# A second fold of the sequence axis in a Fourier mixing, weight loads issued by SyncE, and a new written-out order for the first part

## The chip, the cores and the metric

One Trainium2 chip; the kernel runs on one of its cores. A core has TensorE (PE, the matrix unit), VectorE (DVE), ScalarE (ACT), GpSimd (POOL) and SyncE (SP, which only issues transfers here). The metric is the device time of one execution in microseconds, lower is better; a profiled execution gives a trace beside it.

## What is computed

Two blocks in a row, all in float32. The first is an attention without a softmax over positions (8 batches, 8 heads, 576 positions, head size 64, 128 random features); its output is read as x with 8 batches of 576 rows of 512 columns. The second mixes x by a two-dimensional Fourier transform, of which the real part is kept, and ends in a two-layer perceptron.

```python
def phi(x):
    h = einsum('bhsd,md->bhsm', x, omega) - sum(x * x, -1) / 2
    return exp(h - max(h, -1)) / sqrt(m)
num = phi(q_s) @ (phi(k_s).T @ v);  x = num / (phi(q_s) @ sum(phi(k_s)) + 1e-06)
u = x + real(fft(fft(x, axis=1), axis=2))
un = (u - mean(u)) / sqrt(var(u) + 1e-06)
out = u + maximum(un @ w_ch1, 0) @ w_ch2
```

## The kernel before

The program has two parts. The **first part** does attention, mixing, the narrowing of the two weight matrices (they arrive as float64 and are rebuilt as float32) and the perceptron for the first 512 rows (four "plain" tiles of 128 rows); it also prepares sums of the weights. The **second part** does the perceptron for the other 4096 rows in eight blocks of 512 by a Strassen-like scheme with seven products for eight (L1130 for the first layer, L1309 for the second).

*Attention* runs over 32 pairs of heads (from L512). For each pair q and k are loaded by SP (L347, L350) into two buffers, v into three (L355). PE transposes them (L470) and multiplies them by omega in four 64x64 quarters of its array (L544). DVE takes the maxima (L488), ACT the exponentials e (L505). PE forms the products of the k features with v in quarters (L578), transposes the q features (L470), whose copies qeT ACT takes out of PSUM (L477), and multiplies them by the result in two column halves (L621, L629). DVE adds epsilon, takes the reciprocal and divides (L638, L639, L641) into the tile x of the batch: five slots of 128 partitions, each for two of the nine residues of the position modulo 9, with residue 0 in slot 4 on both partition halves. Three such streams of pairs run interleaved.

*Mixing* of a batch (from L653) starts when its four pairs are in x. The real part of the transform is a cosine product minus a sine product, so rows t and 576 - t are first added for the cosines and subtracted for the sines (L668), then columns in two steps (L670, L674, L687, L694). That leaves three chunks of rows, `fold`. On PE each of four sets (cosine and sine, even and odd columns) contracts the three chunks with a table of 320 frequencies (L712: 12 products of 128x320 a batch); ACT copies each set out of its one PSUM bank (L722). For three groups of rows follow the products over the columns (L739) and the middle column (L744); ACT and DVE take the differences and sums out (L760, L765, L768), and DVE adds one mirror half to x, POOL the other (L776, L777). The results go to a DRAM tensor `us` per batch (L785), the mirrored ones to `uh` (L782), from where one transfer per batch copies them in reverse order into `us` (L803).

```python
for c in range(NC3):
    nc.tensor.matmul(
        yp[:, 0:NK], lhsT=fold[:, c, n, :], rhs=tab[:, c, :],
        start=(c == 0), stop=(c == NC3 - 1),
    )
```

*Weights*: 32 pieces of 512 KB are issued from POOL's queue (L434) into four slabs. For each piece ACT or POOL scales the high words (L409, L407), DVE takes sign and mantissa apart in four instructions (L411, L413, L416, L418), POOL adds the low part (L420).

*Plain tiles*: rows of `us` are read back by SP, normalised on DVE, POOL and ACT (L853 to L867, transposes on PE in L863), multiplied by the first weights (L924), rectified by ACT or DVE (L908, L910), multiplied by the second (L947), and added to u (L960). In the rows' order in `us` the nine residues follow one another, and each 128-row tile is written out by two transfers.

**What sets the order.** Every step is listed as a `Step`: the engine or engines that may do it, a cost, what it waits for, and the buffers and PSUM banks it takes and gives back. `Listing.run` (L159, with `start`, L132) keeps a list of the next step of every stream. For the first part the string `PICKS` says with one character per step which stream is next; where a step names several engines, the one that ends first by the listed costs takes it. For the second part, which has no such string, the step with the earliest start by the listed costs is taken. Each engine then runs its instructions strictly in that order, and SP issues its transfers in that order, waiting where a buffer isn't free.

Of the kernel before, what the change touches and what calls it, by code (L numbers as in the profile page):

```python
# [3 lines left out]

# [9 lines left out]
AF = mybir.ActivationFunctionType  # L14
ALU = mybir.AluOpType
# [12 lines left out]
SLOTS = {1: (0, 0), 2: (1, 0), 3: (0, 1), 4: (1, 1), 8: (0, 2), 7: (1, 2), 6: (0, 3), 5: (1, 3)}  # L28
SLOTS[0] = (0, 4)
# [8 lines left out]
RATE = 190.0  # L38
HOP = 0.15

TURN = 0.1
WIDTH = {"bank": 1, "duo": 2}
FMAX = float(np.finfo(np.float32).max)
# [5 lines left out]
    "00e2ede0ebed3dedebfcdcddfeede3fdfhbi8cdefdebfdgafaggec9hddk0kiij2jejgj7lfffffhcdfffdfcggjehegfi7gjbl"  # L49
    "hbhkjgkkdihfhi7hci7bfiadgkhhjce9didbhhb7gggbfihbbf97acbhbeghefaie8bc7chhhcgfc7cedddh9dd1ccdfif8eggih"  # L50
    "f6g8ejihichdihidfkhfhgjckgigh6eihggiddebd6dcg9eei7cfhei6ddfgihhj78gmkmiidaggjfigdmlg6khhjcj6agghifgg"
    "kh6afejekjkjfigji6j8hjjjiilcj9iegcigdhllkmldjmkkf9j80lca5m7bdai6gfikjaljkika6lhjggic9feikeejhgjij5d7"
    "ldjeafedkdeikjje5g5ielfafej6egkicg8dffgikghjijiee7eeifaaeefhefehdeh7iffd6hb7eeidiedhggiijbkj35fjkjhk"
    "kfgfhkk3h795g4e4i6khchlijigkjji4hlfjfd8lfhlg4mi64bfgjjedjgibk6ijj5cgcijhicgi6lii9fi9lf6ggdijf6bgd8fe"
    "icddchifajihj9fgihgjgi6jbhi6degcbg48ffgfh6ii5kjigihf7jgf9ejggafji7gf7egdfh6ficd6dbhfeeh5addfh5be5bff"
    "c48gai8hg9ageefcj5j7gh6haeeghhjikiehi5mg6lghhl5jjhagd5nglkmlccnjldj9llj45lkjjaemh6gbmlf8f7hgekef6hke"
    "87cldljj8bkhihbhhdc6ffgadkdf7ad5kdbgjhhig6lgcel5mdjedilaidedejihgjegi5ggjhcf5dgc5c775kccdh489j8ddgff"
    "h8cbdgiejkkechjhkkki5gj7kgjjjjfjjjh4i7dhhjjfi4k4h4kjchehg6ihk975g5bfejcehg3dgmggiej6m55bf9igig5h66gg"
    "jjjfiieifh8ege5kdihdlhiheief9k5fimhmcio8hgk7fge5jhgdeifagbgbjeeekhgclgigh7ge8fgefddfaci4icdffhgfid8f"
    "gjffhgihd6gc6cjeelgf3af8hbiccgchgfebg5c9d6ehdfcfeeagghffbhc6f9egchggh6aeehfeekjccbdfafdf50h0gcgabgea"  # L60
    "7fcdcfabg6be8bd4c9dcdcdbcebe6bcgb6cefbacadfeaca7dcdcdchdf9abca66f8dcbd8b98c8aa9c8dd2eabcc87a7b758697"
    "a27277ba9688848aa89a99992b98aa9a287a888729d8a993ba8ac9788aede65bdaacb69ba8ba659b54387a986aaa9baccade"
    "ad9b7bfcecffffde79fe9e6h9bgc3gc3be1eac26e7ebeddbdfeefegd6cdfed2ddf3dadeb3e3cc9dc6c5dbbdcab7b3c72b79b"
    "acbb8abbb679a6a9bb9ab49c7b38a93caa998888888888899888686981458778888888888888841933648786583b59691776"
    "a7c67267761bb4bcb6cc9a679a8aaba3f94df49cbaa675793a9aa88778388a88a93995aa39b94a4954585536126424112222"
    "3333533555523346545266421330442216087635433437704543770334535754155544556455155414437756241426224444"
    "1112032232202111100"
# [39 lines left out]
class Listing:  # L107
# [4 lines left out]
    def __init__(self, buffers):  # L112
        self.free = dict.fromkeys((PE, ACT, DVE, POOL, SP, NONE, PORT), 0.0)
        self.buffers = {name: [0.0] * n for name, n in buffers.items()}
        self.made = {}
        self.moved = 0.0
        self.mode = "whole"
        self.banks = [0.0] * 8
        self.got = None
# [12 lines left out]
    def start(self, step, ready, before):  # L132

        queued = before in step.engines and len(step.engines) == 1
        t = ready[0] if queued else ready[1]
# [15 lines left out]

        def begin(e):
            return max(t, self.free[e] if e != NONE else 0.0, self.free[PORT] if step.on_port(e) else 0.0)

        eng = min(step.engines, key=lambda e: begin(e) + step.engines[e])
        t = begin(eng)
        return t + (TURN if eng == PE and step.mode != self.mode else 0.0), eng

    def run(self, streams, picks=None):  # L159
        todo = []  # L160
        picks = iter(picks or ())

# [14 lines left out]
        while todo:  # L177
            pick = next(picks, None)
            best = None
            for item in todo if pick is None else [todo[int(pick, 36)]]:  # L180
                got = self.start(*item[2:])
                if got is None:
                    continue
                key = got[0] + item[2].bias, item[0]
                if best is None or key < best[0]:
                    best = key, got, item
# [11 lines left out]
            done = end + step.late + (HOP if eng != NONE else 0.0)  # L198
            if step.kb:
                self.moved = max(self.moved, end) + step.kb / RATE  # L200
                done = max(done, self.moved + 1.6)
            for name in step.take:
                if name in WIDTH:
                    n = WIDTH[name]
                    i = self.banks_at(n, begin)[0]
                    self.banks[i : i + n] = [math.inf] * n
                    self.got = Banks(tuple(range(i, i + n)))
                else:
                    self.buffers[name].remove(min(self.buffers[name]))
# [13 lines left out]
def _tables(S, DM):  # L223
# [3 lines left out]
    g, p = np.divmod(np.arange(128), 64)  # L227
    t = np.stack([9 * p + 2 * c + g + 1 for c in range(NL)] + [9 * p], axis=1)
    k = np.concatenate([t[:, c] for c in range(NL)] + [t[:64, NL]])
    w = np.ones(t.shape)  # L230
    w[64:, NL] = 0.0
    turn = (t[:, :, None] * k) % S
    ang = 2.0 * np.pi * turn / S
    cs = np.cos(ang) * w[:, :, None]
    sn = np.where(turn * 2 % S == 0, 0.0, np.sin(ang)) * w[:, :, None]
# [18 lines left out]
def kernel(  # L254
# [19 lines left out]
    NK = NL * 128 + 64  # L274
    KD = DM // 2 + 1
# [48 lines left out]
        bmp=2, slab=4, u=2, unT=1, ht=NFC, ur=1, **{f"vd{i}": 1 for i in range(NV)},  # L324
# [39 lines left out]
    om = att.tile([128, 2, D], F32, name="om", tag="om", bufs=1)  # L364
    for i in range(2):
        nc.sync.dma_start(om[:, i, :], omega[:, :])
# [30 lines left out]
    def narrow(i, dst, raw):  # L397
# [6 lines left out]
        step = Step({ACT: 0.72, POOL: 1.4}, after=(("raw", i),), port=True, bias=1.11)  # L404
# [3 lines left out]
        else:  # L408
            nc.scalar.activation(out=dst, in_=hif, func=AF.Copy, scale=2.0**-112)  # L409
        yield Step(DVE, 0.43, port=True, bias=0.19)  # L410
        nc.vector.tensor_scalar(hi, hi, 0x80000000, None, op0=ALU.bitwise_and)  # L411
        yield Step(DVE, 1.15, port=True, bias=0.36)
        nc.vector.scalar_tensor_tensor(  # L413
            bits, bits, 3, hi, op0=ALU.logical_shift_left, op1=ALU.bitwise_or
        )
        nc.vector.tensor_scalar(hi, bits, 0xFF800000, None, op0=ALU.bitwise_and)  # L416
        yield Step(DVE, 0.7, port=True, bias=-0.99)
        nc.vector.scalar_tensor_tensor(lof, lo, 2.0**-52, hif, op0=ALU.mult, op1=ALU.mult)  # L418
        yield Step(POOL, 1.3, makes=("w", i), give=("slab",), port=True, bias=1.25)
        nc.gpsimd.tensor_tensor(out=dst, in0=dst, in1=lof, op=ALU.add)  # L420

    def weights():
# [4 lines left out]
        for i, (dst, src) in enumerate(parts):  # L427
            if src.dtype == F32:
                yield Step(POOL, 0.6, 4.5, makes=("w", i), kb=256)
                nc.gpsimd.dma_start(dst, src)  # L430
            else:
                yield Step(POOL, 0.6, 5.6, take=("slab",), makes=("raw", i), kb=512)
                raw = slabs.tile([128, CV, 2], U32, name="raw", tag="slab")
                nc.gpsimd.dma_start(raw[:].rearrange("p n two -> p (n two)"), src.bitcast(U32))  # L434
# [6 lines left out]
    us = [dram.tile([S, DM], F32, name=f"us{b}") for b in range(B)]  # L441
    uh = [dram.tile([NL * P, DM], F32, name=f"uh{b}") for b in range(B)]

    def first():

        yield Step(NONE, 3.0)
        yield Step(PE, 0.4, take=("bank",))
        b, omps = got()
        nc.tensor.transpose(omps[:, 0:128], om[:].rearrange("m i d -> m (i d)"), ident[:])
        yield Step(DVE, 0.3, makes="om2", give=(b,))  # L450
        nc.vector.tensor_scalar(om2[:], omps[:, 0:128], SCALE, None, op0=ALU.mult)

    def transposed(src, name, groups, after, makes, give, back=None):
# [3 lines left out]
        for j0, j1 in groups:  # L457
# [3 lines left out]
                0.11 * m,  # L461
# [9 lines left out]
            yield Fork(evicted(dst, b, j0, j1, makes, (j0, j1) == back))  # L471
        return dst

    def evicted(dst, b, j0, j1, makes, back):
        yield Step(ACT, 0.15 + 0.115 * (j1 - j0), 0.1, makes=makes + (j0,), give=(b,), bias=0.08)
        ps = psum_of(b)[:, 0 : 128 * (j1 - j0)].rearrange("q (c p) -> q c p", p=128)
        nc.scalar.activation(  # L477
            out=dst[:, j0:j1, :], in_=ps[:, :, ::-1] if back else ps, func=AF.Copy
        )

    def softmax(n, ts, num, b, es):
# [3 lines left out]
        yield Step(DVE, 0.15 + 0.27 * num, bias=-0.56)  # L485
# [10 lines left out]
        for i, one in enumerate(b):  # L496
            if num == 4 or not i:
                yield Step(
                    ACT, 1.18 if num == 4 else 0.65, 0.0, take=(size,),
# [12 lines left out]
    def attn(n):  # L512
# [16 lines left out]
        def pairs_of(js, *ts):  # L529
# [4 lines left out]
                0.235 * len(js),  # L534
# [52 lines left out]
        def keep():  # L587
            step = Step({DVE: 0.3, ACT: 0.35}, take=("kv",), give=(kvb,), makes=("kv", n))
# [10 lines left out]
            lambda r: feature(R + r),  # L599
            "qeT",  # L600
            ((0, 1), (1, 5), (5, R)),
            lambda j0, j1: tuple(("e", n, t) for t in sorted({place(R + j)[0] for j in range(j0, j1)})),
            ("qeT", n),
            lambda j0, j1: {1: ("e1",), 5: (), R: ("e", "e")}[j1],
            (5, R),
        )
        yield Step(
            PE,
            1.23,
# [5 lines left out]
        ndb, ndp = got()  # L615

        for i, order in enumerate(((2, 1, 4, 3, 7, 8, 5, 6), (2, 1, 4, 3, 7, 8, 5, 6))):
            for r in order:
# [828 lines left out]
```

## Time and profile before

Three runs took 1225.72 us in the median (1225.62 to 1227.41); the profiled execution's span is 1222.5 us, its mean granted TensorE clock 0.997.

| engine | busy us | share of the span | instructions |
|---|---|---|---|
| PE | 1188.2 | 97% | 12705 |
| PE weight loads | 1064.3 | 87% | 12705 |
| DVE | 746.0 | 61% | 1522 |
| ACT | 458.2 | 37% | 1432 |
| POOL | 383.5 | 31% | 451 |

Some groups that the change touches, with busy time and mean duration of one record:

| line, engine, what | count | busy us | mean ns |
|---|---|---|---|
| L712 PE products with the cosine and sine tables | 192 | 56.1 | 440 |
| L744 PE middle column | 144 | 15.3 | 236 and 192 |
| L641 DVE division into x | 32 | 26.4 | 825 |
| L505 ACT exponentials | 576 | 158.9 | 396 |
| L477 ACT copies qeT, 512 and 128 columns | 64 and 32 | 36.5 and 9.3 | 612 and 289 |
| L722 ACT copies y | 32 | 14.1 | 442 |
| L420 POOL sum of the weights' two parts | 32 | 43.7 | 1367 |
| L434 POOL issue of the weight loads | 32 | 19.0 | 594 |
| L668 DVE and POOL first fold | 12 and 4 | 15.2 and 9.4 | 1265 and 2348 |

How to read it: a float32 product of PE shows as two records, so L712's 96 products are 192. Records of PE overlap, so that the mean duration is longer than the spacing of two in a row; busy time counts overlap once. The kernel's page also has the chain of work that ended last, followed back from the last instruction: 92% of the span lies on PE there. L1130 and L1309 have 32% and 29% of it, L712 has 4%.

### The profile page before, as it was taken

The numbers are of one execution on the slowest core, as the hardware profiler recorded it, in microseconds if no ns is written. First come the engines' busy times: TensorE is split into PE (matmuls) and PEld (weight loads), VectorE is DVE, ScalarE is ACT, GpSimd is POOL, SyncE is SP. The second block draws the span as 40 slices with busy tenths as digits, with TensorE's granted clock in tenths as the row PEclk, the third lists the DMA queues.
The fourth block names the chain that finished last, engine by engine and source line by source line (L and its number), as shares of the span: only waits on it lengthen the run. The fifth ranks groups of instructions, "written<-read, shape, count | busy, mean of one in ns | idle before, by whom it ended". The sixth has DMA issues, their size and how long they took to land.

```text
span 1222.5 us, 31614 instructions
## 1 busy us (share of the span) xinstructions
PE 1188.2 (97%) x12705; PEld 1064.3 (87%) x12705; DVE 746.0 (61%) x1522; ACT 458.2 (37%) x1432; POOL 383.5 (31%) x451
## 2 busy tenths in 40 slices
PE   6989899999999999999999999999999999999997
PEld 5778878878878777999899899899899899899897
DVE  4889899897674664384384285185276266267255
ACT  6867767666653521222222212222222222222211
POOL 3443443531111013322422422431431521431421
PEclk9999999999999999999999999999999999999999
DMA  9564654736653334195196096186186277267255
GB/s 262 155 205 146 200 177 144 218 91 210 175 194 130 123 114 162 55 304 168 35 304 188 10 309 186 30 284 193 50 258 201 59 248 218 61 212 255 61 175 172
DMA packets 149058, 206.02 MB, mean 169 GB/s; under 512 B 49328, under 2 KB 62896, under 8 KB 148912
## 3 DMA queue, kind: packets, MB, share of 16 engines
q1 hardware_dynamic: 144224, 187.15, 49.8%
q0 software_dynamic: 4608, 16.78, 4.3%
q8 instruction: 101, 1.65, 0.6%
q14 instruction: 45, 0.37, 0.1%
q10 hardware_dynamic: 80, 0.07, 0.0%
HBM read 172.23 MB, written 35.91 MB: 170 GB/s over the span
## 4 chain that ended last, share of the span: by engine, by line
PE 92%; DVE 3%; ACT 3%; DMA 0%; issue 0%; SPq 0%; DVEq 0%; ACTq 0%
PE banks L1130 32%; PE banks L1309 29%; PE banks L924 5%; PE banks L947 5%; PE banks L470 4%; PE banks L544 4%; PE banks L712 4%; PE banks L578 3%; PE banks L621 3%; ACT e L505 2%; PE banks L739 2%; PE banks L863 1%; DVE nmx L488 1%; PE banks L744 1%; ACT kqT L477 1%; PE banks L629 1%
## 5 line engine op out<-in xcount | busy, mean ns | idle before, releaser
L1116 DVE CUSTOM_DVE_ANT_0 hid<-banks,s 128x256 f32<-128x256 f32 x192 | 79.7, 423 | 254.9 <-PE banks L1130 254.9
L1309 PE MATMUL banks<-wl,sums 128*128 128x128 f32 x1792 | 220.3, 275 | 0.0
L1309 PEld LDWEIGHTS banks<-wl,sums 128*128 128x128 f32 x1792 | 210.5, 192 | 1.0
L505 ACT ACTIVATE e<-banks,nmx 128x128 f32<-128x128 f32 x576 | 158.9, 396 | 42.4 <-DVE nmx L488 42.4
L1144 ACT ACTIVATE s<-banks 128x256 f32<-128x256 f32 x192 | 73.6, 383 | 257.6 <-PE banks L1130 257.6
L1130 PE MATMUL banks<-unT,w 128*128 128x256 f32 x704 | 167.3, 379 | 0.0
L1130 PEld LDWEIGHTS banks<-unT,w 128*128 128x128 f32 x704 | 132.7, 190 | 17.9 <-issue 0.5
L1284 ACT ACTIVATE s<-banks 128x128 f32<-128x128 f32 x168 | 46.5, 277 | 236.9 <-PE banks L1309 175.5
L1130 PE MATMUL banks<-tt,w1s 128*128 128x256 f32 x512 | 126.3, 379 | 0.0
L1197 POOL TENSOR_TENSOR hs<-hid 128x256 f32<-128x256 f32 x64 | 46.4, 726 | 200.2 <-DVE hid L1116 173.6
L1130 PEld LDWEIGHTS banks<-tt,w1s 128*128 128x128 f32 x512 | 97.2, 190 | 13.3
L488 DVE TENSOR_REDUCE nmx<-banks 128x8 f32<-128x1024 f32 (+1 forms) x96 | 88.3, 953 | 32.2 <-PE banks L544 27.2
L1309 PE MATMUL banks<-wl,hid 128*128 128x128 f32 x768 | 98.9, 275 | 0.0
L1309 PEld LDWEIGHTS banks<-wl,hid 128*128 128x128 f32 x768 | 94.0, 192 | 1.4 <-DMA wl<-w2l 0.2
L1289 DVE TENSOR_TENSOR part<-banks,s 128x128 f32<-128x128 f32 x168 | 48.7, 290 | 75.3 <-PE banks L1309 74.2
L1197 POOL TENSOR_TENSOR hs<-hid,hs 128x256 f32<-128x256 f32 x64 | 46.4, 725 | 118.7 <-issue 93.3
L544 PE MATMUL banks<-om,kqT 64*64 64x128 f32 x2304 | 76.8, 275 | 4.7 <-ACT kqT L477 2.0
L1130 PE MATMUL banks<-unT,w1s 128*128 128x256 f32 x320 | 80.7, 379 | 0.0
L544 PEld LDWEIGHTS banks<-om,kqT 64*64 64x64 f32 x2304 | 63.8, 134 | 16.1 <-issue 4.2
L857 POOL TENSOR_TENSOR rstd<-rstd,mhalf 128x1 f32<-128x1 f32 x36 | 29.0, 806 | 153.6 <-DVE rstd L855 137.8
L1309 PE MATMUL banks<-wl,hs 128*128 128x128 f32 x576 | 74.9, 275 | 0.4 <-DVE part L1289 0.4
L420 POOL TENSOR_TENSOR w<-w,raw 128x512 f32<-128x512 f32 x32 | 43.7, 1367 | 99.5 <-DVE raw L418 80.5
(115 smaller groups left out, 1998.1 us busy)
## 6 DMA issues: line engine op xcount, KB each, us to landing
wl<-w2l SPq DMA_DIRECT2D x392, 256.0 KB, 3.7
raw<-in_moe_w_ch_dram POOLq DMA_DIRECT2D x32, 512.0 KB, 5.2
kq<-in_k_dram SPq DMA_DIRECT2D x32, 288.0 KB, 3.8
kq<-in_q_dram SPq DMA_DIRECT2D x32, 288.0 KB, 4.5
vd<-in_v_dram SPq DMA_DIRECT2D x32, 288.0 KB, 4.9
out_dram<-ur SPq DMA_DIRECT2D x68, 128.0 KB, 2.4
u<-us SPq DMA_DIRECT2D x32, 256.0 KB, 4.0
ur<-us SPq DMA_DIRECT2D x32, 256.0 KB, 3.1
```

Of the source, the lines that this page charges most:

```text
L470: nc.tensor.transpose(ps[:, (j - j0) * 128 : (j - j0 + 1) * 128], src(j), ident[:])
L488: nc.vector.tensor_reduce(nmx[:, :, 0:num], pps[:, :, 0 : MF * num].rearrange("p b (c m) -> p b c m", m=MF), axis=AX.X, op=ALU.max, negate ...
L505: nc.scalar.activation(out=e[:, c + (i if num == 1 else 0), :], in_=pps[:, i, MF * c : MF * c + MF], func=AF.Exp, bias=nmx[:, i, c : c + 1],)
L544: nc.tensor.matmul(pps[cols, c, MF * m : MF * m + MF], lhsT=kqT[rows, j, cols], rhs=om2[rows, :],)
L712: nc.tensor.matmul(yp[:, 0:NK], lhsT=fold[:, c, n, :], rhs=tab[:, c, :], start=(c == 0), stop=(c == NC3 - 1),)
L924: nc.tensor.matmul(hp[:, 0:TP], lhsT=w1[:, dc, 128 * fc : 128 * fc + 128], rhs=unTs[key][:, dc, :], start=(dc == 0), stop=(dc == NDC - 1),)
L947: nc.tensor.matmul(yp[:, 0:DM], lhsT=hs[fc][:, 128 * i : 128 * i + 128], rhs=w2[:, fc, :], start=(fc == 0), stop=(fc == NFC - 1),)
L1116: nc.vector._custom_dve(TENSOR_ADD_SAT, out=o, in0=ps, in1=sb, s0=FMAX, s1=0.0)
L1130: nc.tensor.matmul(ps[:, 0:HT], lhsT=left(dc), rhs=right(dc), start=start and dc == 0, stop=(dc == D2 - 1), skip_group_check=True,)
L1144: nc.scalar.activation(out=s[:], in_=ps[:, 0:HT], func=AF.Copy)
L1197: nc.gpsimd.tensor_tensor(out=o, in0=l, in1=r, op=op)
L1309: nc.tensor.matmul(ps[:, 0:128], lhsT=left[:, f], rhs=wls[j, i, n][:, f], start=start and f == 0, stop=(f == 3), skip_group_check=True,)
```

## The change

- **Tables and mixing.** After the first fold (t with 576 - t) the two chunks that hold the residues are also added and subtracted (new L740), which pairs t with 288 - t: even frequencies need only the sum, odd ones only the difference. `h` grows by a chunk. The cosine and sine tables get 160 columns for each of sum and difference and 320 for residue 0. Four sets become two groups that take two PSUM banks each; a group has four products of 128x160 and two of 64 rows by 320 columns, one on each half of the array's rows. ACT copies a group out in three pieces. The middle column takes four small products of 64 (or 32) output rows.
- **Attention.** qeT's copies put the positions into the order that the new fold needs; each of the three becomes two ACT instructions with more dimensions. The division may be done by ACT as ten scaled copies.
- **Row order.** `us` is one tensor with the rows in their natural order; results are written there with strides, mirrored ones by eight reversed transfers a batch for one. Tiles of 128 rows are contiguous when they are read and written out.
- **Weights.** The loads move from POOL's queue to SP's; the signs get a tile of their own; the last sum may run on DVE. Omega is loaded from ACT's queue.
- **Order.** A `Clock` holds the constants of the listing, one set for each part; many listed costs of the first part have new values. `PICKS` is new, and a character from the upper range also says that the step goes to the other engine than the one that would end first. First folds, last folds and final sums may each run on DVE or POOL.

```diff
-            for c in range(NC3):
+            plus = slice(0, HK), slice(HK, NK)
+            for m in range(2):
+                for c, cols in ((0, plus[1 - n]), (NL, plus[n])):
+                    nc.tensor.matmul(
+                        yp[:, m, cols],
+                        lhsT=fold[:, c, 2 * n + m, :],
+                        rhs=tab[:, cols],
...
+            for m in range(2):
+                rows = slice(64 * m, 64 * m + 64)
                 nc.tensor.matmul(
-                    yp[:, 0:NK],
-                    lhsT=fold[:, c, n, :],
-                    rhs=tab[:, c, :],
+                    yp[:, m, 0:NK],
+                    lhsT=fold[rows, 1, 2 * n + m, :],
+                    rhs=tab[rows, NK : 2 * NK],
...
+            step = Step({DVE: 0.9, POOL: 1.5}, port=True)
+            yield step
+            eng = nc.gpsimd if step.eng == POOL else nc.vector
+            for dst, o in ((NC3, ALU.add), (1, ALU.subtract)):
+                eng.tensor_tensor(
+                    out=h[:, dst, 0 : 2 * QD + 1],
+                    in0=h[:, 0, 0 : 2 * QD + 1],
+                    in1=h[:, 1, 0 : 2 * QD + 1],
+                    op=o,
+                )
...
-                yield Step(POOL, 0.6, 5.6, take=("slab",), makes=("raw", i), kb=512)
+                yield Step(SP, 0.5, 4.2, take=("slab",), makes=("raw", i), kb=512)
                 raw = slabs.tile([128, CV, 2], U32, name="raw", tag="slab")
-                nc.gpsimd.dma_start(raw[:].rearrange("p n two -> p (n two)"), src.bitcast(U32))
+                nc.sync.dma_start(raw[:].rearrange("p n two -> p (n two)"), src.bitcast(U32))
...
-        nc.sync.dma_start(om[:, i, :], omega[:, :])
+        nc.scalar.dma_start(om2d[:, D * i : D * i + D], omega[:, :])
...
+        step = Step({DVE: 0.74, ACT: 1.2}, give=(ndb,), makes=("x", b, pr), bias=-0.07)
+        yield step
+        if step.eng == ACT:
+            for i in range(2):
+                for c in range(5):
+                    nc.scalar.activation(
+                        out=dst[:, i, c], in_=nd[:, i, c, 0:D], func=AF.Copy, scale=rden[:, i, c : c + 1]
+                    )
+            return
...
-            nc.vector.tensor_scalar(hi, hi, 0x80000000, None, op0=ALU.bitwise_and)
+            nc.vector.tensor_scalar(sign[:], hi, 0x80000000, None, op0=ALU.bitwise_and)
...
-        yield Step(POOL, 1.3, makes=("w", i), give=("slab",), port=True, bias=1.25)
-        nc.gpsimd.tensor_tensor(out=dst, in0=dst, in1=lof, op=ALU.add)
+        step = Step({POOL: 1.25, DVE: 0.61}, makes=("w", i), give=("slab",), port=True, bias=1.25)
+        yield step
+        eng = nc.gpsimd if step.eng == POOL else nc.vector
+        eng.tensor_tensor(out=dst, in0=dst, in1=lof, op=ALU.add)
...
-            for i in range(NC3):
+                g, odd = divmod(i, 2)
+                rows = slice(64 * odd, 64 * odd + 64) if g else slice(0, 128)
+                k1 = HK * odd + k0 + NK * g
                 nc.tensor.matmul(
-                    ab[0:np_, 1, KD : KD + 1],
-                    lhsT=cs[:, i, rows],
-                    rhs=mid_t[:, i, :],
+                    ab[w * odd : w * odd + w, 1, KD : KD + 1],
+                    lhsT=cs[rows, k1 : k1 + w],
+                    rhs=mid_t[rows, 1 if g else NL * (1 - odd), :],
...
+                nc.sync.dma_start(uh[b][:, 2 - slot], u)
...
-            nc.sync.dma_start(
-                us[b][nh : 2 * nh, :].rearrange("t (i d) -> i t d", i=4),
-                uh[b][nh - 1 :: -1, :].rearrange("t (i d) -> i t d", i=4),
-            )
+            for s in range(2):
+                for n, r in enumerate(MIRROR):
+                    back = uh[b][4 * (1 - s) + n].rearrange("e t (i d) -> (e t) i d", i=4)
+                    nc.sync.dma_start(
...
```

## The prediction, written before the changed kernel was run

> **What bounds the kernel now.** I read first the page's busy shares in 40 slices, then the busy time of each engine by stage, then the chain of work and PE's waits. The change touches only what is issued before the first L1130 (464.27 us in the chain), so the stages are cut there. Columns: busy us (instructions) of PE, its weight loads, DVE, ACT, POOL; then clock, DMA share, GB/s.
>
> ```profile
> 0.00:8.00 8.00, 1.69 (x6) 1.05 (x7) 0.29 (x1) 1.88 (x2) 4.23 (x15) 1.00 0.67 211
> 8.00:50.00 42.00, 36.05 (x965) 31.49 (x966) 29.88 (x48) 33.95 (x117) 12.83 (x12) 1.00 0.89 242
> 50.00:100.00 50.00, 44.47 (x957) 38.77 (x956) 44.25 (x87) 37.17 (x118) 22.63 (x21) 0.97 0.60 173
> 100.00:150.00 50.00, 45.48 (x921) 39.40 (x919) 45.42 (x91) 36.33 (x118) 21.06 (x21) 1.00 0.58 171
> 150.00:200.00 50.00, 45.94 (x924) 40.06 (x925) 46.64 (x97) 36.24 (x113) 19.35 (x18) 1.00 0.54 162
> 200.00:464.27 264.27, 263.62 (x3899) 210.18 (x3900) 189.56 (x400) 141.95 (x459) 59.81 (x58) 1.00 0.49 155
> 464.27:1215.00 750.73, 750.35 (x5037) 702.94 (x5037) 389.19 (x800) 170.65 (x507) 243.57 (x309) 1.00 0.54 170
> ```
>
> PE is the bound: it lacks 0.4 us in the last 750 us and 0.65 us from 200 to 464. Only before 200 us does it stand idle, 6.3 us in the first row and 20.1 in the next four; in those four DVE is busy 166.2 of 192 us. The waits of PE name what ends that idle time (total us, times, longest us):
>
> ```profile
> PE banks L470 <- ACT e L505: 6.5, 7, 1.9
> PE banks L449 <- DMA om<-in_omega_dram: 3.5, 1, 3.5
> PE banks L578 <- ACT e L505: 3.2, 4, 1.4
> PE banks L470 <- DMA kq<-in_k_dram: 2.1, 1, 2.1
> ```
>
> ACT's exponentials (L505) wait in turn on DVE's maxima (L488; 42.4 us in the table of waits). So early on a ring PE, DVE, ACT sets the pace; later PE alone. The chain (start, us, what) gives prices for the products of the mixing:
>
> ```profile
> 52.65 3.43 PE banks L712 x12
> ...
> 56.95 3.23 PE banks L712 x12
> ...
> 62.49 0.56 PE banks L744 x6
> ...
> 65.64 0.30 PE banks L744 x6
> ...
> 106.32 1.81 PE banks L712 x6
> ...
> 109.55 1.62 PE banks L712 x6
> ```
>
> One f32 product is two records. Six L712 records last 1.62 us, but 1.81 right after L578's 64x64 products (L544 too, at 206.06): a change of array shape costs 0.19.
>
> **What the Trainium skill says.** "TensorEngine Tiling (Array Packing)", Key Properties: tiles of the array run in parallel, and changing the tiling mode drains TensorE. The trace agrees with both: 32 records of L544 (eight sets of four 64x64 tiles) take 1.03 us, 0.129 a set, where one whole 128-column record (L1309, 16.25/144) takes 0.113; and the 0.19 above. Its Gotcha 1 says that row tiles write different PSUM banks, which the new half-row products do; no product of 64 rows by 128 columns is in this trace. "SBUF — State Buffer", two separate sides: DVE (two SBUF inputs) and GpSimd exclude each other for a whole instruction. The trace agrees: L777 on DVE is 0.42 us in the median, 2.59 at most, beside GpSimd's L776 and L777. So moving work from DVE to GpSimd frees less than its count.
>
> **The change part by part.** Counts are from the order of instructions per engine of both kernels.
>
> *Second fold, PE.* Per batch L712's twelve 320-column products (24 records, 3.43 + 3.23 = 6.66 us) become eight of 160 columns and four of 64 rows by 320 columns. Records of 128 columns take 0.113, of 320 columns 1.62/6 = 0.270; on that line 160 columns take 0.139. 16 x 0.139 = 2.22. The half-row records, two at a time, with the 0.016 that L544's sets lose: 4 x 0.286 = 1.14. Sum 3.36, saving 3.30, eight times 26.4 us. Against it the array changes shape after each half-row pair: 16 x 0.19 = 3.0. The change into it isn't shown; into 64x64 sets it is free (32 records of L544 last 1.03 to 1.10 us behind whole-array products): 0, at most 3.0. The middle column: L744 (0.56 + 0.56 + 0.30 = 1.42 a batch) becomes four small products, two by columns and two by quarters. Priced as L621's pairs (32 records 1.08 us, 0.0675 a pair), two pairs each are 0.27, plus 0.19 for the way back: 3 x 0.46 = 1.38, so 0, with bounds of 2 us gained and 5 lost (a change of shape in front as well). **PE work: 437.2 - 26.4 + 3.0 = 413.8 us** before the second part. The order shows 78 returns from quarters to the whole array for 54; the 24 more are the 24 middles, counted above.
>
> *Fold arithmetic, DVE/POOL.* Sixteen more pairs of 257-wide sums: 12 instructions on DVE at L776's 0.42 (+5.0 us), 20 on POOL at 0.8 (+16).
>
> *Engine choices.* DVE: 20 of 32 divisions (L641, 0.825) leave: -16.5; 15 sums of w2 (L1017, 0.69): -10.4; 5 first folds (L668, 1.265): -6.3; final sums (L776/777) -5.0; L687 -1.4; the other way 32 relus (L908, 0.288) +9.2, 9 weight sums (L420's work at 0.69) +6.2, copies +0.6. With the folds **DVE -18.6**, about 15 of it before the 16th pair of heads, partly because one batch's mixing falls behind that point. ACT: 200 scaled copies of 64 columns for the divisions; none is shown, L505's 128 columns take 158.9/576 = 0.276 back to back, so between 0.1 and 0.276, say 0.14: +28. Six qeT copies for three: 64 x 0.14 + 128 x 0.38 (L1144's 256 columns) - 45.8 = +12. y copies +2.6, relus -8.9, others -1: **ACT +33**. POOL: its DMA issues (L434, 19.0) go; with folds, first folds (+12), final sums (+10), w2 sums (+20), weight sums (-12), others (+4): **POOL +30**. Against a first part of 434 us that is DVE 337 (78%), ACT 320 (74%), POOL 170 (39%): all below PE.
>
> *Waits that are new.* A division on ACT waits for DVE's reciprocal (L639) with exponentials queued behind it on ACT, and with the pair of PSUM banks held meanwhile, which the next products of PE may want; each sequence fold now takes two neighbouring banks until three copies (0.7 us at 0.28 to 0.38 each, overlapping) are done, not one bank for L722's 0.44. Neither is in this trace. At worst every one of the 20 divisions and 16 folds stops PE for a copy, 0.4 us: 14 us; nothing is gained by them. I take 0 beyond the idle time below, because the order places other heads' products between; the sign tile's single buffer is written and read by DVE alone and costs nothing.
>
> *SyncE.* 32 raw weight loads move from POOL's queue to SP's, which is in order: a raw load that waits for a slab now holds back the q, k and v loads and the stores of u listed behind it. Of stores of u there are 64 for 40, of reversed copies 64 for 8: with the weights 32 + 24 + 56 = 112 issues, at the 0.43 of a kq issue 48 us more on SP, spread over 434. A pair of heads takes 464/32 = 14.5 us, the q load lands 4.5 us after issue; I take nothing, and put the other end into the rivals. Omega leaves SP (L366, 0.39 + 0.41): the first q and k arrive 0.9 us sooner, and PE starts on them 0.9 sooner.
>
> *Second part.* Same instructions and counts on PE; half as many stores of out. Hidden by PE (750.35 of 750.73). The last 7.5 us keep their three small stores.
>
> *Idle time of PE.* First stage 6.3 - 0.9 = 5.4. From 8 to 200 us: L712's share there is 21.3 of 56.1 us, so 9 us of PE's saving; DVE's load falls by about as much or more, ACT's (75%) rises. Floor 8 (the ramp at the start stays), ceiling 20 + 9 = 29; I take 13, since the ring is shortened at two of its three engines. Later PE has less filler and waits a little: 0.65 becomes 2. Sum 20.4.
>
> **First part 413.8 + 20.4 = 434.2 for 464.3: -30.1.** The profiled span is 1222.5; the other runs (1225.6 to 1227.4, median 1225.7) lie some 3 above, so 1195.6, forecast 1195.
>
> **Rivals.**
> 1. *The ring keeps the pace before 200 us.* For it: 87% DVE there, and longer copies on ACT in the ring (qeT). Against: DVE is relieved. Idle there 29: 413.8 + 5.4 + 29 + 2 = 450.2, -14: 1211.
> 2. *Half-row products don't overlap.* For it: no row here. Against: L544's sets of four. 16 x (1.08 - 0.57) = 8.2 more: 1204.
> 3. *The ring loosens fully.* Idle falls to 5.4 + 5 + 0.6 = 11: 1186. Speaks for it that DVE falls to 78% throughout; against, that 8 to 50 us alone now holds 6 us of ramp.
> 4. *Slower: SP's queue is blocked by weight loads.* SP already waits 80 us for kq's buffer (L347) and 58 + 38 for vd's. From 30/32, or 0.95 us per raw load seen by PE, the gain is eaten; at 1.4 us, 45 us come back: 1240. PE would wait at the first transposes for DMA kq. Against: SP has 14.5 us per pair, and only 0.6 us of such q waits today.
> That the change does nothing is excluded by the counts of the order.
>
> **How the numbers follow.** Forecast 50%, rival 1 15%, rival 2 12%, rival 3 17%, rival 4 6%. A difference over 0.2% (2.5 us) can be told from none. Range 1183 to 1211: it takes in rivals 2, 3 and half of 1 and the shape-change bounds. Faster 93%, within 0.2% 1%, slower 6%.
>
> **What would show it.** Products of the sequence fold between 27 and 30 us in all (35 to 38 with rival 2); first L1223 near 434 us; PE idle before 200 us near 18; DVE some 19 us less, ACT 33 more, POOL 30 more; the second part unchanged within 2 us. Wrong if PE waits long for kq or vd, or if idle grows where PE was saved.

## The result and the profile after

The changed kernel took 1212.26 us in the median of four runs (1210.28 to 1213.61), the kernel before 1226.57 beside it (1225.62 to 1228.14): a ratio of 0.9887 (95% interval 0.9870 to 0.9904). It is faster, by 14 us where 31 were forecast. The profiled span is 1209.2 us. All medians here and below are of fast runs; one run of E3, 1224.46 us at a clock of 0.948, is slow and left out.

Busy time by stage of the kernel after, cut at its first L1223 (442.78 us), columns as in the prediction:

```profile
0.00:8.00 8.00, 3.15 (x26) 2.85 (x30) 0.29 (x1) 2.65 (x4) 0.85 (x10) 1.00 0.84 225
8.00:50.00 42.00, 36.69 (x979) 30.81 (x974) 33.11 (x54) 36.98 (x140) 16.63 (x12) 1.00 0.77 221
50.00:100.00 50.00, 45.83 (x1004) 37.75 (x997) 43.86 (x97) 44.43 (x175) 21.42 (x18) 1.00 0.63 178
100.00:150.00 50.00, 47.18 (x1053) 40.70 (x1057) 41.12 (x94) 44.17 (x173) 19.81 (x19) 1.00 0.65 194
150.00:200.00 50.00, 49.25 (x1070) 43.68 (x1063) 45.15 (x102) 45.43 (x172) 22.43 (x20) 1.00 0.60 183
200.00:442.78 242.78, 237.21 (x3616) 188.02 (x3615) 159.76 (x376) 145.16 (x546) 84.38 (x81) 1.00 0.52 157
442.78:1200.00 757.22, 749.98 (x5009) 701.03 (x5008) 373.27 (x795) 170.16 (x505) 239.49 (x308) 1.00 0.52 169
```

PE's idle time from 8 to 200 us is now 5.3 + 4.2 + 2.8 + 0.7 = 13 us for 20; the ring of PE, DVE and ACT did loosen, though ACT now stands at 88 to 91% from 50 to 200 us. But two rows are worse than before: 5.6 us of idle time after 200 us, and over 7 us in the last row, where there were 0.4. The span divides so (us, first part up to the first product of the second):

| | before | forecast | after | missing |
|---|---|---|---|---|
| PE busy, first part | 437.1 | 413.8 | 419.3 | 5.5 |
| PE idle, 0 to 8 us | 6.3 | 5.4 | 4.9 | -0.5 |
| PE idle, 8 to 200 us | 20.1 | 13 | 13.0 | 0 |
| PE idle, later in the first part | 0.7 | 2 | 5.6 | 3.6 |
| second part | 758.3 | 758.3 | 766.4 | 8.1 |

(Idle time here is the gap between records of PE, so it differs by tenths from the row's busy time.) Half of what is missing lies at one place. PE's waits of the kernel after begin with a line that had no counterpart, and SyncE's own waits show one of 10.0 us at the store of out that the next paragraphs are about:

```profile
PE banks L1223 <- ACT s L1237: 7.1, 1, 7.1
SPq L925 <- DVE ur L1052: 10.0, 1, 10.0
```

The chain at that place (start, us, what), kernel after:

```profile
446.01 5.31 DMA us<-uh
...
451.37 0.39 ACT s L1237
...
451.80 28.23 PE banks L1223 x118
```

ACT's first copy of the second part writes into memory that the first part had used, so it waits for the last transfers of x (E1 and E5 below test this). SyncE's queue shows why they are late (start, duration, line, x instructions), kernel after and then before:

```profile
443.70 0.36 SPq L925 DMA_DIRECT2D out_dram<-ur  x1
444.14 1.11 SPq L893 DMA_DIRECT2D us<-x  x2
445.36 8.06 SPq L910 DMA_DIRECT2D us<-uh  x8
453.53 7.27 SPq L1306 DMA_DIRECT2D wl<-w2l  x13
```

```profile
452.27 0.46 SPq L785 DMA_DIRECT2D us<-x  x1
452.84 0.65 SPq L803 DMA_DIRECT2D us<-uh  x1
465.02 1.16 SPq L840 DMA_DIRECT2D out_dram<-ur  x2
```

In the new listing the last plain tile's store of out (L925) stands ahead of the last batch's stores of x (L893). It waits 10.0 us for DVE's last sum (L1052), which is the last work of the first part, and the two stores of x wait behind it, though their data are there some 10 us earlier (E1 below issues them at 433.33, not at 444.14). Before, the store of out was last.

### The profile page after: what moved, and what is told of

It is laid out like the page before. It is cut to its first block, busy times and chain, and to the rows that moved or that the text cites. A ratio compares the mean times of both kernels' runs of the same rounds, so it can differ in the third digit from the quotient of the medians.

```text
span 1209.2 us, 32038 instructions
## 1 busy us (share of the span) xinstructions
PE 1173.3 (97%) x12753; PEld 1048.5 (87%) x12753; DVE 699.3 (58%) x1522; ACT 489.5 (40%) x1709; POOL 406.3 (34%) x466
## 4 chain that ended last, share of the span: by engine, by line
PE 85%; ACT 8%; DVE 3%; DMA 2%; issue 2%; POOL 0%; SPq 0%; ACTq 0%; DVEq 0%
PE banks L1223 32%; PE banks L1402 29%; PE banks L1039 5%; PE banks L1016 4%; PE banks L504 3%; PE banks L586 3%; ACT e L547 3%; ACT x L693 2%; PE banks L620 2%; PE banks L828 2%; PE banks L668 1%; PE banks L956 1%; ACT kqT L515 1%; PE banks L780 1%; ACT qeT L521 1%
## 5 line engine op out<-in xcount | busy, mean ns | idle before, releaser
L547 ACT ACTIVATE e<-banks,nmx 128x128 f32<-128x128 f32 x576 | 167.3, 467 | 28.3 <-DVE nmx L530 28.2
L1223 PE MATMUL banks<-unT,w 128*128 128x256 f32 x704 | 167.5, 379 | 0.0
L1223 PEld LDWEIGHTS banks<-unT,w 128*128 128x128 f32 x704 | 132.8, 190 | 18.0 <-issue 0.5
L1223 PE MATMUL banks<-tt,w1s 128*128 128x256 f32 x512 | 127.4, 381 | 7.1 <-ACT s L1237 7.1
L1223 PEld LDWEIGHTS banks<-tt,w1s 128*128 128x128 f32 x512 | 97.6, 191 | 21.0 <-ACT s L1237 7.5
L586 PE MATMUL banks<-om,kqT 64*64 64x128 f32 x2304 | 82.6, 277 | 5.5 <-ACT kqT L515 2.1
L1223 PE MATMUL banks<-unT,w1s 128*128 128x256 f32 x320 | 82.3, 385 | 0.0
L586 PEld LDWEIGHTS banks<-om,kqT 64*64 64x64 f32 x2304 | 65.8, 134 | 17.8 <-issue 4.4
L1402 PEld LDWEIGHTS banks<-wl,hs 128*128 128x128 f32 x576 | 70.0, 192 | 0.9 <-DVE part L1382 0.6
L1223 PEld LDWEIGHTS banks<-unT,w1s 128*128 128x128 f32 x320 | 61.8, 194 | 8.9
```

The lines of the kernel that those rows point to most:

```text
L547: nc.scalar.activation(out=e[:, c + (i if num == 1 else 0), :], in_=pps[:, i, MF * c : MF * c + MF], func=AF.Exp, bias=nmx[:, i, c : c + 1],)
L586: nc.tensor.matmul(pps[cols, c, MF * m : MF * m + MF], lhsT=kqT[rows, j, cols], rhs=om2[rows, :],)
L1223: nc.tensor.matmul(ps[:, 0:HT], lhsT=left(dc), rhs=right(dc), start=start and dc == 0, stop=(dc == D2 - 1), skip_group_check=True,)
L1402: nc.tensor.matmul(ps[:, 0:128], lhsT=left[:, f], rhs=wls[j, i, n][:, f], start=start and f == 0, stop=(f == 3), skip_group_check=True,)
```

## Experiments

Those on the changed kernel are, but for the first, built on E1; their "part" figures come from one profile each. First part, second part and PE's busy time in the first part, in us:

| kernel | median us | ratio to before (95%) | first | second | PE busy |
|---|---|---|---|---|---|
| E1 last store of out issued last | 1201.69 | 0.9798 (0.9780 to 0.9815) | 442.2 | 756.5 | 419.9 |
| E5 reversed copies behind it again | 1202.01 | 0.9799 (0.9779 to 0.9820) | 441.4 | 757.0 | 417.7 |
| E2 all divisions on DVE | 1211.15 | 0.9871 (0.9854 to 0.9888) | 450.7 | 756.8 | 418.3 |
| E3 half-row products on the whole array | 1202.83 | 0.9806 (0.9782 to 0.9829) | 445.9 | 756.5 | 423.2 |
| E4 before, half the sequence products | 1216.82 | 0.9930 (0.9907 to 0.9954) | 454.7 | 758.7 | 420.6 |
| E6 weight loads on POOL again | 1209.31 | 0.9876 (0.9855 to 0.9898) | 450.9 | 756.8 | 421.3 |
| E7 all divisions on ACT | 1230.66 | 1.0039 (1.0019 to 1.0060) | 477.3 | 756.5 | 435.2 |
| E8 nine weight sums on POOL again | 1211.13 | 0.9889 (0.9866 to 0.9911) | 451.0 | 756.5 | 421.5 |
| E10 before, weight loads on SP | 1224.57 | 0.9993 (0.9982 to 1.0003) | 463.6 | 757.8 | 436.6 |
| E11 before, stores of x behind | 1230.27 | 1.0042 (1.0025 to 1.0058) | 464.0 | 764.4 | 436.9 |

**E1, the order of the last stores.**

```diff
+        if t == NPLAIN - 1:
+            held.append(lambda: store_rows(t, ur[:]))
+            return
...
+    for store in held:
+        store()
```

> The changed kernel, with one transfer moved: SP issues the store of the last plain tile behind the last batch's stores of u and its eight reversed copies, not in front of them. Theory 1 (the wait of 7.1 us ahead of the second part comes from those stores of x standing in SP's queue behind a store that waits for DVE's last sum, so that the memory of x comes free late): the wait goes to under 1 us, the span falls by 7 to 8 us, time about 1204 to 1205. Theory 2 (PE would have waited there for something else anyway, for the reloaded weights of the second layer or for the slabs): the wait stays within 2 us of 7.1 under another name and the time stays at 1210 to 1212.

Measured: 10.6 us less than the kernel after, 9.9 of them in the second part; PE's wait at its start is gone. In SyncE's queue of E1 the stores of x start at 433.33 and the store of out comes last:

```profile
433.33 1.12 SPq L893 DMA_DIRECT2D us<-x  x2
434.55 8.01 SPq L910 DMA_DIRECT2D us<-uh  x8
443.07 0.36 SPq L925 DMA_DIRECT2D out_dram<-ur  x1
```

**E5, which of the transfers holds the memory.** Only the eight reversed copies are issued behind the store of out again; the stores of x stay ahead.

> As the run with the store of the last plain tile moved, but it is put between the last two stores of x and the eight reversed copies, so the copies are still late by the same 12 us while the reads of x are early. If the late reads of x are what holds the second part's memory: as the other run, about 1204 to 1205. If the reversed copies themselves hold it (the trace names them as what ACT's first copy waited for): the wait of 7 us stays and the time is 1210 to 1212.

Measured: no difference from E1 (1202.01 and 1201.69). So late copies alone make no stall: it needs the late stores of x, although the chain names a copy (us<-uh) as the transfer waited for. Whether the copies lengthen the wait once the stores are late isn't tested.

**E11, the same cost put into the kernel before.** The last store of x and its reversed copy are issued behind the last store of out.

```diff
+                if (b, c) == (B - 1, NL):
+                    behind.append(lambda: nc.sync.dma_start(us[b][r0 : r0 + np_, :], u))
+                    return
...
+        if t == NPLAIN - 1:
+            for store in behind:
+                store()
```

> The kernel before, with only the order of the last stores on SyncE changed: the last batch's last store of x and its reversed copy are issued behind the last plain tile's store of out, as they stand in the new kernel. Theory (the place of that store on SyncE's in-order queue makes the stall at the second part's start, and nothing else of the change is needed for it): TensorE waits 5 to 9 us at the first product of the second part, where it waited under 1 us, and the time grows by 6 to 10 us, to 1232 to 1236 us, all of it after the first part. Rival (the stall needs the new kernel's ring or its longer reversed copies): no wait above 2 us there, and a time within 2 us of before.

Measured: slower by 4.5 us, the first part unchanged, the second 6.1 us longer in the profiled execution. The mechanism holds, and here the profile itself names the store of x as what ACT's first copy waited for:

```profile
ACT s L1159 <- DMA us<-x: 15.8, 1, 15.8
PE banks L1145 <- ACT s L1159: 3.1, 1, 3.1
```

The wait of PE is smaller than expected, 3.1 us. From the issue of the late store of x (466.10) to ACT's first copy (468.61) it is 2.5 us here, in the kernel after 7.2 (444.14 to 451.37), where two stores and eight copies follow one another; which of these makes it longer stays open. The rest of the 6.1 is not waiting. The windows at that place show what it is (last three columns: clock, DMA share, GB/s):

```profile
468.00:470.00 2.00, 0.95 (x2) 0.84 (x3) 1.34 (x3) 0.66 (x2) 0.00 (x0) 0.54 0.22 59
470.00:472.00 2.00, 2.00 (x6) 1.58 (x5) 1.97 (x5) 0.38 (x1) 0.00 (x0) 0.50 0.29 87
472.00:474.00 2.00, 2.00 (x6) 1.55 (x6) 2.00 (x4) 0.00 (x0) 0.00 (x0) 0.50 0.58 172
474.00:476.00 2.00, 2.00 (x9) 1.69 (x8) 1.97 (x4) 0.00 (x0) 0.00 (x0) 0.75 1.02 349
476.00:478.00 2.00, 2.00 (x11) 1.77 (x10) 1.32 (x4) 0.77 (x2) 0.73 (x1) 1.00 1.02 357
```

After the pause PE runs at half its clock: 6 records in 2 us where there are 11 later. From 468 to 476 that costs 0.5 + 2 x 0.5 + 2 x 0.5 + 2 x 0.25 = 3.0 us, and with the 3.1 of waiting this is the 6.1. The kernel after has the same behind its 7.1 us: 0.50 from 452 to 456, 0.78 from 456 to 458, 2.4 us lost. So E1's 9.9 us are 7.1 of waiting and 2.4 of clock, to within half a microsecond. The Trainium skill, "TensorE: Matmul & The Clock Gate", Part 1: The HAM clock gate, says that an idle stretch of about 3.4 us halves PE's clock, and that it takes about as long a busy one to get it back. The traces agree that the clock is halved after a pause and returns after some microseconds of work, but shorter pauses were enough here: 3.1 us in E11, and 2.0 us in the kernel before itself, where PE waits for an exponential until 72.16:

```profile
PE banks L621 <- ACT e L505: 2.0, 1, 2.0
```

```profile
72.00:74.00 2.00, 1.84 (x38) 1.84 (x40) 1.48 (x5) 2.00 (x10) 0.00 (x0) 0.62 1.04 390
74.00:76.00 2.00, 2.00 (x70) 1.88 (x70) 1.45 (x4) 1.46 (x6) 0.00 (x0) 0.53 0.54 201
```

That pause costs another 0.7 + 0.9 = 1.6 us of clock. Not each pause of that size does it: one of 1.87 us, at 177 us of the same trace, leaves the clock at 1.00.

**E2 and E7, where the divisions go.** In E2 the 20 divisions that ACT does go back to DVE (`if False:` for `if step.eng == ACT:`), in E7 all 32 go to ACT (`if True:`).

> The store of the last plain tile is last, as in the first of these runs, and all 32 divisions into x are done by DVE (0.82 us each), in the places where ACT had 20 of them. ACT loses 43 us of busy time, DVE gains 16. If ACT, busy 89 to 91% between 50 and 200 us in the changed kernel, holds the early stretch: faster by 3 to 8 us than the first of these runs. If DVE holds it (the reason for moving the divisions): slower by 3 to 8 us. If PE alone bounds it: within 2.5 us.

> The changed kernel with the store of the last plain tile last, and the other 12 divisions into x done by ACT too. DVE loses 10 us, ACT gains some 26. By what the run with all of them on DVE showed (16 us more on DVE cost 9.5 us of time), a DVE bound alone would give 4 to 6 us faster than the run with only the store moved. If ACT, at 90% from 50 to 200 us, is by now just as full: slower by 3 to 10 us.

Measured: E2 is 9.5 us slower than E1 and E7 29 us. PE's idle time in the first part is 32.4 us in E2 and 42.0 in E7, for 22.3 in E1; E2's largest wait is

```profile
PE banks L504 <- DVE x L697: 6.6, 1, 6.6
```

and E7's waits lie on ACT:

```profile
PE banks L504 <- ACT e L547: 9.7, 9, 2.8
```

E7's clock is 0.987 over the span, which makes its PE busy time longer as well. In E2 two pauses of PE (6.6 us at 64 us and 2.9 us at 139 us) are more than the whole increase of its idle time before 200 us, 13.4 to 22.2: like E6 and E8 below, E2 moves work inside an order that was made without it, so it doesn't price DVE's load alone.

**E3, the half rows.** The half-row products and the middle column run over all 128 rows, with the table of residue 0 halved to make up for it.

```diff
-                rows = slice(64 * m, 64 * m + 64)
+                rows = slice(0, 128)
```

> The store of the last plain tile is last, as in the first of these runs, and the products of 64 rows by 320 columns (and those of the middle column) use all 128 rows, with the table for residue 0 halved, since both row halves hold the same data: same result, no change of the array's shape to half rows or to quarters in the mixing. Theory A (the half-row pairs overlap, but the shape changes around them eat the saving): sequence products 5 to 6 us more in their own lines, other lines as much less, total within 2.5 us of the first of these runs. Theory B (the half-row pairs are worth their 8 us, and shape changes cost what was forecast, 0.19 on the way back only): 5 us slower or more. Theory C (shape changes are the missing 5.5 us of PE): faster by 2 to 5 us.

Measured: 1.1 us slower than E1, and the intervals overlap. PE's records give the prices. The timeline of PE (start, us, line, x records), kernel after and then E3, where lines are one higher:

```profile
61.89 0.81 PE L790 MATMUL banks<-cs_sb,fold 64*128 64x320 f32 x4
62.63 0.66 PE L504 MATMUL banks<-ident,e 128*128 128x128 f32 x4
```

```profile
64.25 1.24 PE L791 MATMUL banks<-cs_sb,fold 128*128 128x320 f32 x4
65.33 0.60 PE L505 MATMUL banks<-ident,e 128*128 128x128 f32 x4
```

From one start to the next, four half-row records take 0.74 us, four over the whole array 1.08: they overlap, and rival 2 is out. Record by record, the first pair takes 0.470 us behind the plain products and the second 0.269, as much as one record over the whole array (1.077/4): the pair overlaps fully, and the way into half rows costs 0.20. Measured from end to end of records, the four transposes behind them cost 0.588 us behind half rows and 0.437 behind the whole array; behind half rows the first plain products, 0.641 for 0.445, and the 160-column products, 0.741 for 0.542, pay the same. The sets of 64x64 tiles (L586) start free in both, mostly 0.270. So a return to the whole array costs 0.15 to 0.20. Over all 16 groups the half rows take 11.8 us and E3's products 17.2; the middle column goes the other way, 9.3 and 7.05. A version with the half rows kept and only the middle column over all rows needs another table; it wasn't tried.

**E4, only less PE work in the old order.** Of the twelve sequence products of a batch six are left out of the kernel before.

> The kernel before, with six of a batch's twelve products of the sequence axis left out (chunk 1 of every set, and the third chunk of the odd-column sets), so its mixing is incomplete; its order and all else stay. PE loses 48 products of 0.56 us each, about 27 us, as much as the second fold saves there. Theory PE (PE's work before the second part becomes time one for one, whatever the order): about 27 us faster than before, 1199 to 1201. Theory ring (before 200 us, where 38% of these products lie, DVE sets the pace and the saving returns as idle time): about 17 us faster, 1209 to 1211, with 8 to 10 us more idle time of PE before 200 us.

Measured: L712 takes 25 us less, the time falls by 9.0 us in the median (9.4 in the first part). PE's idle time rises from 27.0 to 34.1, and in one stage the clock falls:

```profile
100.00:150.00 50.00, 43.99 (x827) 38.91 (x827) 40.58 (x87) 33.52 (x109) 19.20 (x19) 0.90 0.52 155
```

So in the old order, with DVE and ACT as full as before, two thirds of the saving on PE are lost: 7 us to idle time, some 8 to longer records elsewhere, of which the lower clock there explains about 50 x 0.1 = 5.

**E6 and E10, the queue of the weight loads.** E6 gives them back to POOL in the changed kernel, E10 gives them to SP in the kernel before (`nc.gpsimd.dma_start` and `nc.sync.dma_start` exchanged in one line).

> The changed kernel with the store of the last plain tile last, and the 32 weight loads issued from POOL's queue at the same places in the order, as in the kernel before. If SP's queue, held by those loads, costs time (late q and k: the waits of PE for DMA kq and the idle time that the trace calls issue, some 6 us): faster by 2 to 5 us than the run with only the store moved. If their move to SP is what relieves POOL and DVE (19 us of issue on POOL, which shares a port with DVE): slower by 2 to 6 us. If neither is on the path: within 2 us.

> The kernel before, with one part of the change alone: the raw weight loads are issued by SyncE at the same places instead of by GpSimd, in the old order with all twelve sequence products. Theory (the gain of 7.6 us that this move showed in the new kernel is GpSimd's queue set free, and the first part of the kernel before leans on GpSimd too): faster by 2 to 7 us, so 1220 to 1224 us, with the gain in the idle of TensorE between 8 and 200 us. Rival A (the loads block SyncE's queue, rival 4 of the prediction): slower by 5 us or more. Rival B (the move pays only because the new order was chosen with it in place; in the old order it frees nothing): within 2 us of before.

Measured: E6 is 7.6 us slower than E1 by the medians, 9.6 by the ratios to before; E10 is not told apart from before. The chain of E6 shows the loss in one piece:

```profile
250.76 0.46 POOL x L878
...
251.46 0.36 POOL x L879
...
252.05 0.64 POOL x L878
252.69 0.62 POOL x L879
253.31 8.22 DMA raw<-in_moe_w_ch_dram
...
261.55 0.02 ACT w L438
...
262.11 1.12 ACT x L693 x5
...
263.28 2.36 PE banks L504 x9
```

On POOL's queue the load comes behind four final sums and is issued at 253.31, where SP in E1 issued the same one, the last of the 32, at 244.75; it lands 8.2 us later, against 5.2 in the median of the kernel before, and why isn't followed here. ACT's scaling of that piece (L438) waits 5.6 us for it at the head of ACT's queue, ten copies of a division (L693) stand behind it, and PE waits 5.3 us for these; then its clock is 0.50 until 268. In the kernel before, where no division is on ACT, the same move is worth nothing. The first part of E6 is 8.7 us longer than E1's; this pause and some 2.3 us of clock behind it (263.3 to 268 at half) make 7.6 of that. The gain is thus for the most part not POOL's 19 us of issuing, but one place in an order that counts on the load being early.

**E8, nine weight sums back on POOL** (`eng = nc.gpsimd`).

> The changed kernel with the store of the last plain tile last, and the nine weight sums that DVE does (0.68 us each) done by POOL (1.33 us), as the kernel before does all of them. DVE loses 6.2 us, POOL gains 12 and is busy 40 to 45% there. If DVE's count of work holds the early stretch: faster by 2 to 4 us than the run with only the store moved. If the port that the two share gives it back (a POOL sum shuts DVE's two-input instructions out for 1.3 us): within 1.5 us or slower.

Measured: 9.4 us slower than E1 by the medians, 11.2 by the ratios to before. Here too one pause makes most of it; PE waits for a q that is issued late, and the chain in front of it shows why:

```profile
PE banks L504 <- DMA kq<-in_q_dram: 5.1, 1, 5.1
```

```profile
261.76 2.55 POOL w L454 x2
...
265.19 1.05 POOL x L879
...
266.26 0.60 SPq L885
...
266.91 4.68 DMA kq<-in_q_dram
```

Two weight sums stand on POOL ahead of a final sum (L879), SyncE's store of that sum (L885) waits for it, and the load of q stands behind the store: it is issued at 266.91, in E1 at 259.01. This is the mechanism of the kernel after's stall once more, in the middle of the first part. Behind the pause the clock is at half until 277.6, some 2.9 us lost.

## Why the prediction was right and wrong

- **Wrong: "Second part. Same instructions and counts on PE; half as many stores of out. Hidden by PE", taken as 0.** It cost 8.1 us in the profiles; removing its cause in E1 gives 9.9. The instructions are the same, but the first of them waits for the first part's memory, and the step counted SyncE's issues without looking at which of them stands ahead of which at the end. Kernel E11 shows that the place in the queue is enough for a stall, though for a smaller one. In the kernel after the step "SyncE ... I take nothing" failed at this place alone; its other end, rival 4, is out: the move of the weight loads helps the changed kernel (E6) and doesn't hurt the old one (E10), and PE waits for q only 1.2 us in all in the kernel after. E8 shows how near that end lies: there one store holds a q load back and costs 5.1 us.
- **Wrong in size: "PE work 413.8", measured 419.3.** By end-to-end spacing L712 falls from 54.1 us to 30.7 in L780 and L790. The working priced the products at 8 x 3.36 = 26.9, and took 0 for the change of shape into half rows, with at most 3.0 as its bound. That change costs 16 x 0.20 = 3.2, of which 0.5 comes back because a pair takes 0.269 and not 0.286: 2.7 us; 160 columns take 0.147 for 0.139: 1.0. The way back to the whole array, 3.0 in the working, is paid in 9 of 16 cases only, because the others go on to 64x64 tiles or other packed products: about 1.6. L712 itself was 54.1 before, 0.8 more than the working took. Together that leaves 1.5 of the 5.5. The middle column, taken as 0 with a bound of 2 gained, gains 2.1 (11.4 to 9.3), which hides it. So the 5.5 lie in lines that the change keeps, and which the working took as unchanged: L544 to L586 +5.1, L470 to L504 +3.0 and the plain tiles' products (L924 and L947) +1.9, the 1.6 of the way back among them, against 2.1 gained at L578 and L621. Read in the order of the records, the transposes (L470, L504) come in 60 groups before and in 81 after. Those that follow products on a part of the array (quarters, column halves, half rows), each 0.15 dearer in the median, are 43 and 55, which makes 1.8 of the 3.0. At L586 a group behind transposes costs nothing extra in the median; seven groups before 132 us are 0.34 to 1.05 us too long, 3.6 in all: short stops inside a group. What stops them isn't shown.
- **Wrong in size: "Later PE has less filler ... 0.65 becomes 2", measured 5.6**, in small waits none over 1.6 us; E1 has 3.9 with the same order. The direction was right.
- **Right: the ring loosened in part.** Idle time from 8 to 200 us is 13, as taken; rivals 1 (29) and 3 (11 with the start) are out. That the number is met so closely is luck: 13 was chosen between a floor of 8 and a ceiling of 29, not worked out. E2, E4 and E7 fit the picture: with DVE's divisions given back, or ACT loaded further, or PE's work alone cut, the gain goes into idle time. Which part of the change loosened the ring isn't shown, since no run makes one of them alone in the old order but E4 and E10. E7 shows no room left on ACT in this order.
- **Right in direction, and for ACT by luck: the loads of the engines.** DVE was to lose 18.6 us, ACT to gain 33, POOL 30. In the stages up to the second part ACT rises by 31 and POOL by 26. In ACT's sum two errors cancel: the 200 scaled copies of the divisions take 43 us, not 28, and all else together falls by 12 where it was to rise by 5. DVE falls by 33 (356.0 to 323.3), more than forecast; 6 us of it are the four instructions that take sign and mantissa apart, which got shorter (84.2 to 78.1 us for 128) and were taken as unchanged, and another 6.6 are its final sums: 28.7 us for 48 (L776, L777) become 17.1 for 36, a loss of 11.6 where 5.0 were taken for the count alone. The mean of one falls too, most of all at L777's 128 rows (920 ns to 485). So moving these sums to POOL freed more of DVE than their count, against what the working expected.
- **Right: the overlap of the half rows** (rival 2 refuted), and omega's move: PE's idle time before 8 us is 4.9, taken as 5.4.

E1 takes 1201.7, 0.6% above the forecast: the first part, 442.2 us for 434.2, was read rightly in its main terms, and the largest missing term was at its end. E1, at a ratio of 0.9798 (0.9780 to 0.9815), is the best of all versions here.

## What to carry to other kernels

Where the order of an in-order queue changes, follow it to its last instructions: a store that waits for the very last result must not stand ahead of transfers that free memory for the next part, nor a store that waits for a busy engine ahead of a load that PE needs (E8). Add the clock to a pause of PE: here 3.0 and 2.4 us were lost behind pauses of 3.1 and 7.1 us, and 1.6 behind one of 2.0. And price a single move of an engine inside the order it was made for: the same move was worth some 8 us in one order and nothing in the other.

## What the runs showed of the hardware

- **The clock after a pause.** PE worked at half speed for 4.7 to 6.0 us after waits of 7.1 us (kernel after), 3.1 us (E11) and 5.3 us (E6), and for some 3.4 us after a wait of 2.0 us (kernel before, at 72 us). In all the stages shown of the kernel after's first part, where no pause is longer than 1.84 us, the clock is 1.00.
- **Changes of the array's shape.** Into half rows 0.20 us (0.470 less 0.269), back to the whole array 0.15 to 0.20 (0.588 for 0.437, 0.741 for 0.542), on to 64x64 tiles nothing (0.270 both ways). Two half-row records of 320 columns take together what one over the whole array takes, 0.269 us.
- **Reversed copies.** The issue of a reversed transfer keeps SyncE busy for 0.64 us in the median of 64 (2.66 at most; the last eight take 8.06 together), those of the kernel before, eight times as large (512 KB), for 0.66 (median of 8).
